# Two of the seven down products made jointly for two column sets, with x of the second half parked in DRAM and Exp and Silu run in order

## The chip, the cores and the metric

The kernel runs on one core of one Trainium2 chip. The time of a run is the device time of one execution in microseconds. I quote medians of the fast runs. PE is TensorE, DVE is VectorE, ACT is ScalarE, POOL is GpSimd and SP is SyncE, whose queue issues the DMAs here. A profiled execution has a "span", from the first to the last instruction that the profile counts. It is about 1.7 us shorter than the time of the same execution (727.4 against 729.12 for the kernel before). The core alone is used, so there is no second die to compare with.

## The reference, cut to what matters

```python
x = A_x                                   # 2048 x 1024, bf16
xn = _layernorm(x)
# A: linear attention, 32 heads of 32
qkv = xn @ wqkv
pq, pk = phi(q), phi(k)                   # phi(t) = where(t > 0, t + 1, exp(t)) + 1e-6
o = (pq @ (pk^T v)) / (pq . sum(pk) + 1e-6)
s = o @ wo
# B: gated feed-forward, F = 3584
h = silu(xn @ w_gate) * (xn @ w_up)
g = silu(h @ w_down)                      # the "down" product: 2048 x 3584 by 3584 x 1024
return x + s * g
```

There are two activation functions with a lookup table, Exp (in phi, for q and k) and Silu (for gate and for the final g).

## The kernel before: the parts that the change touches

The kernel works in two halves of 1024 rows. In each half it makes q, gate and up products, then the down product in four column sets of 256 columns. Every product is a Strassen-type scheme: a 2 x 2 block product is made with seven block products instead of eight, from sums of the weights and sums of the activations. In a column set of the down stage each of the seven is a chain of 14 matmuls of 512 columns into a PSUM bank (PSUM, `ps` in the traces, is the memory that the matmuls write; the kernel uses eight banks of 128 x 512 values).

```python
class Set:                                 # one column set: seven products (cut)
    def step(self, m):
        if m == 1:
            a = balloc(True); self.grp(1, a, True); self.put1(a)
        elif m == 5:
            e = balloc(True); self.grp(5, e, True); self.put5(e)
        elif m == 6:
            self.grp(6, self.b, False)
            self.c = balloc()
            tt([bank_r[self.b], self.s5.r], [bank_r[self.c]], ps[self.c][:, :],      # the DVE add that
               self.s5.ap(F32), ALU.add)                                             # product 3 waits for
        elif m == 3:
            self.grp(3, self.c, False); self.out(0, 1, self.c)
        ...                                # [cut: 2, 7, 4]
```

(The code here is condensed, and comments are mine.) In q, gate and up, products 1 and 5 of two neighbouring sets were already made jointly, as one product of twice the width that is itself split into seven "inner" products (class `Joint`, steps a to d). The down stage made all seven products of each set by itself:

```python
            dset = Set(dops, keep(gv, ACT.Silu), dd_ring)
            seq = "1 5 6 2 7 3 4"
            if link:                       # last set of the first half: woven into the turn to the second half
                seq = "1 5 X 6 nj1a 2 nj1b 7 nj1c 3 nj1d nj5a 4 nj5b n2_0 nj5c n6_0 n2_1 nj5d n6_1"
```

The kernel plans itself at build time. Each operation is recorded with an estimated duration, and a list scheduler fixes the order of every engine's queue. `LEAD=12.0` says how many microseconds ahead of its deadline a load may be issued. `WINDOW=6` says from how many matmul groups, counted from the first one not yet placed, the planner may choose TensorE's next. Once built, every queue runs strictly in order.

```python
def build_kernel(nc, A_x, ..., out, WINDOW=6, NWARM=14, NPE=4, LEAD=12.0):
```

## Time and profile before

| | before |
|---|---|
| time, median of 3 runs | 729.06 us (728.75 to 730.27) |
| PE busy | 712.1 of 727.4 us |
| DVE, ACT busy | 612.7, 400.2 us |
| loads of an activation table | 10, of 1283 ns each |
| DMA | 94.02 MB |

These are lines from the first and fourth part of the page of the kernel before: the busy time of each engine with its instruction count, and the shares of the chain of work that ended last.

```profile
span 727.4 us, 10731 instructions
...
PE 712.1 (98%) x3928; PEld 372.0 (51%) x3942; DVE 612.7 (84%) x1443; ACT 400.2 (55%) x759; POOL 14.4 (2%) x35
...
PE 92%; DVE 4%; ACT 1%; DMA 1%; issue 0%; SPq 0%; DVEq 0%
```

TensorE is busy for 98% of the span, and the chain runs through it for 92%. Where the small remainder sits is seen by stretches. Each row below gives a window in us, its length, then the busy time (and the count) of PE, PE weight load, DVE, ACT and POOL, the granted clock, the DMA share and GB/s.

```profile
337.00:420.00 83.00, 83.00 (x393) 38.22 (x391) 59.22 (x118) 14.67 (x26) 0.00 (x0) 1.00 0.66 166
420.00:445.00 25.00, 24.59 (x142) 13.50 (x141) 22.95 (x60) 19.20 (x34) 0.00 (x0) 1.00 0.51 150
520.00:540.00 20.00, 18.83 (x103) 9.60 (x102) 19.98 (x49) 15.48 (x32) 0.00 (x0) 1.00 0.34 107
636.00:721.00 85.00, 84.84 (x394) 38.28 (x391) 49.35 (x95) 14.53 (x26) 0.00 (x0) 1.00 0.55 132
```

337 to 420 is the down stage of the first half, 420 to 445 the turn, 636 to 721 the down stage of the second half. In the two down stages PE is idle for 0.00 and 0.16 us. In 420 to 445 the gap is 0.41 us. The waits of PE after 200 us, from the view of waits (engine, what it made, what it waited for, total us, how often, the longest):

```profile
PE ps L226 <- DVE TM L360: 1.1, 1, 1.1
PE ps L219 <- DVE ps L360: 0.9, 2, 0.5
PE ps L219 <- ACT ps L350: 0.9, 1, 0.9
PE ps L219 <- ACT TM L350: 0.8, 2, 0.6
PE ps L219 <- DVE W L360: 0.2, 1, 0.2
```

Together 3.9 us, of which the 1.1 us in the first line is the tail of the program. So the kernel is bound by the columns that TensorE streams, and only fewer columns can gain much.

The timeline of PE (start us, length us, engine, line, what, form, count) gives what a 512-column product costs:

```profile
636.07 18.29 PE L219 MATMUL ps<-H,W 128*128 128x512 f16 x84
654.20 3.18 PE L219 MATMUL ps<-P,W 128*128 128x512 f16 x14
657.22 1.03 PE L219 MATMUL ps<-H,W 128*128 128x512 f16 x4
```

From 636.07 to 657.22 there are 98 matmuls: 21.15 / 98 = 0.216 us each. (The length of a row includes the modelled end of its last matmul, so the distance from start to start is what counts. Some records can be missing, which is why I count over whole products.)

### The profile page before, as it was taken

The numbers are of one execution on the slowest core, as the hardware profiler recorded it, in microseconds if no ns is written. First come the engines' busy times: TensorE is split into PE (matmuls) and PEld (weight loads), VectorE is DVE, ScalarE is ACT, GpSimd is POOL, SyncE is SP. The second block draws the span as 40 slices with busy tenths as digits, with TensorE's granted clock in tenths as the row PEclk, the third lists the DMA queues.
The fourth block names the chain that finished last, engine by engine and source line by source line (L and its number), as shares of the span: only waits on it lengthen the run. The fifth ranks groups of instructions, "written<-read, shape, count | busy, mean of one in ns | idle before, by whom it ended". The sixth has DMA issues, their size and how long they took to land.

```text
span 727.4 us, 10731 instructions
## 1 busy us (share of the span) xinstructions
PE 712.1 (98%) x3928; PEld 372.0 (51%) x3942; DVE 612.7 (84%) x1443; ACT 400.2 (55%) x759; POOL 14.4 (2%) x35
## 2 busy tenths in 40 slices
PE   7999999999999999999999999999999999999996
PEld 3544445555555555554444455555555555544442
DVE  5999968989989998888656989999999888875662
ACT  3777654887659666663111267666966756511111
POOL 3111000000000000000000000000000000000000
PEclk9999999999999999999999999999999999999999
DMA  9444235144255343325179655234615344448732
GB/s 295 110 87 102 45 115 174 59 127 149 81 164 156 112 148 114 108 59 151 54 180 253 159 152 160 60 115 119 176 59 187 104 129 131 131 123 188 183 99 51
DMA packets 135668, 94.02 MB, mean 129 GB/s; under 512 B 32960, under 2 KB 131520, under 8 KB 135616
## 3 DMA queue, kind: packets, MB, share of 16 engines
q1 hardware_dynamic: 135616, 93.34, 45.8%
q8 instruction: 31, 0.51, 0.3%
q14 instruction: 21, 0.17, 0.1%
HBM read 75.50 MB, written 10.62 MB: 118 GB/s over the span
## 4 chain that ended last, share of the span: by engine, by line
PE 92%; DVE 4%; ACT 1%; DMA 1%; issue 0%; SPq 0%; DVEq 0%
PE ps L219 92%; DVE H L360 2%; DMA H<-in_A_wqkv_dram 1%; DVE W L360 1%; DVE ps L360 1%; ACT TM L350 1%; ACT L350 0%; SPq L363 0%; DVE TM L360 0%; PE ps L226 0%; ACT ps L350 0%; ACT X L350 0%; DVE H L737 0%; ACT H L350 0%; DVEq L243 0%
## 5 line engine op out<-in xcount | busy, mean ns | idle before, releaser
L219 PE MATMUL ps<-X,W 128*128 128x512 f16 (+1 forms) x1232 | 267.6, 358 | 1.9 <-DVE ps L360 0.9
L350 ACT ACTIVATE TM<-ps 128x512 f16<-128x512 f32 (+2 forms) x345 | 183.6, 553 | 128.5 <-PE ps L219 126.2
L219 PE MATMUL ps<-H,W 128*128 128x512 f16 (+2 forms) x1162 | 250.4, 369 | 0.3
L360 DVE TENSOR_TENSOR W<-W 128x256 f16<-128x256 f16 (+5 forms) x440 | 176.8, 439 | 8.8 <-DMA W<-in_B_w_down_dram 5.8
L219 PEld LDWEIGHTS ps<-H,W 128*128 128x128 f16 (+1 forms) x1168 | 113.9, 98 | 123.4 <-DVE W L360 0.3
L219 PEld LDWEIGHTS ps<-X,W 128*128 128x128 f16 (+1 forms) x1232 | 119.7, 98 | 100.5 <-ACT ps L350 2.1
L360 DVE TENSOR_TENSOR ps<-ps,TM 128x256 f32<-128x256 f32 (+1 forms) x234 | 124.2, 533 | 25.7 <-PE ps L219 23.9
L350 ACT ACTIVATE ps<-ps 128x512 f32<-128x512 f32 (+1 forms) x164 | 81.7, 499 | 108.2 <-PE ps L219 103.6
L219 PE MATMUL ps<-P,W 128*128 128x512 f16 (+1 forms) x496 | 100.1, 329 | 0.6 <-ACT TM L350 0.6
L350 ACT ACTIVATE H<-ps 128x512 f16<-128x512 f32 (+1 forms) x126 | 75.0, 604 | 42.7 <-PE ps L219 42.6
L360 DVE TENSOR_TENSOR H<-H 128x1024 f16<-128x1024 f16 (+4 forms) x106 | 66.5, 642 | 2.2 <-DMA H<-in_A_wqkv_dram 1.9
L219 PEld LDWEIGHTS ps<-P,W 128*128 128x128 f16 (+1 forms) x496 | 48.4, 98 | 31.7 <-ACT TM L350 0.9
L360 DVE TENSOR_TENSOR H<-H,TM 128x512 f16<-128x512 f16 x112 | 44.7, 418 | 15.1 <-ACT H L350 14.9
L219 PE MATMUL ps<-W 128*128 128x256 f16 (+1 forms) x278 | 56.5, 289 | 0.4 <-ACT TM L350 0.2
L350 ACT ACTIVATE TM<-TM 128x512 f16<-128x512 f32 (+1 forms) x61 | 38.0, 627 | 33.9 <-DVE TM L360 33.8
L360 DVE TENSOR_TENSOR TM<-ps,TM 128x512 f32<-128x512 f32 (+1 forms) x60 | 40.8, 680 | 16.2 <-PE ps L219 15.4
L219 PEld LDWEIGHTS ps<-W 128*128 128x128 f16 (+1 forms) x278 | 26.2, 98 | 26.9 <-ACT TM L350 1.5
L219 PE MATMUL ps<-H,X 128*128 128x512 bf16 (+1 forms) x133 | 32.2, 379 | 2.8 <-ACT X L350 1.6
L219 PE MATMUL ps<-TM,W 128*128 128x256 f16 (+1 forms) x138 | 27.8, 283 | 0.1
L360 DVE TENSOR_TENSOR H<-ps,TM 128x512 f16<-128x512 f32 (+1 forms) x35 | 23.9, 683 | 2.3 <-PE ps L219 1.8
L219 PE MATMUL ps<-H,P 128*128 128x512 bf16 (+1 forms) x94 | 23.1, 379 | 0.1
L219 PEld LDWEIGHTS ps<-H,X 128*128 128x128 f16 x136 | 12.7, 98 | 18.3 <-ACT X L350 2.0
(81 smaller groups left out, 392.8 us busy)
## 6 DMA issues: line engine op xcount, KB each, us to landing
W<-in_B_w_down_dram SPq DMA_DIRECT2D x16, 896.0 KB, 6.1
W<-in_B_w_gate_dram SPq DMA_DIRECT2D x12, 1024.0 KB, 5.4
W<-in_B_w_up_dram SPq DMA_DIRECT2D x12, 1024.0 KB, 5.4
W<-in_A_x_dram SPq DMA_DIRECT2D x16, 256.0 KB, 3.0
H<-in_A_wqkv_dram SPq DMA_DIRECT2D x8, 512.0 KB, 8.1
H<-r_scratch SPq DMA_DIRECT2D x32, 128.0 KB, 3.3
W<-m_scratch SPq DMA_DIRECT2D x4, 1024.0 KB, 5.5
s_scratch<-TM SPq DMA_DIRECT2D x32, 128.0 KB, 2.7
```

What stands on the lines that cost most here:

```text
L219: last = h.matmul(o, l, r, start=st, stop=sp, skip_group_check=True)
L350: q = PL.op("act", reads, writes, lambda h: h.activation(o, i, func, **kw), nel(o) / (1000.0 if "bias" in kw or not isinstance(kw.get("sca ...
L360: return dve(reads, writes, lambda h: h.tensor_tensor(o, a, b, op), nel(o), 1.92 if fast else 0.96)
```

## The change

The intent is to save columns. In the down stage, products 1 and 5 of two column sets become one joint product each, made in seven inner products of 7 matmuls of 256 columns. For a pair of sets that is 98 matmuls of 256 columns in place of 56 of 512. It needs inner sums of the weights, inner sums of the activations (`tj_first`, `tj_second`, `tj_last`), and room for both. The room comes from the place `P` that held x of the second half: that is written to DRAM early and loaded back at the turn. A term of product 4 is now made once for two sets. And since Exp and Silu alternate at the turn, `PL.table` forces the runs of the two functions to stay in program order. Some further edits are not shown. Among them, several small tiles moved, and the planner gives vector and scalar work recorded from `END_D` on a deadline 4 us behind its place in TensorE's work instead of 30.

The diff below is cut to its core; comments are mine.

```diff
+    def table(self, o, tab):
+
+        o.tab = tab
+        if self.run and self.run[0].tab != tab:
+            self.past, self.run = self.run, []
+        o.after = [p for p in ([self.run[0]] if self.run else self.past) if p not in o.preds]
+        for p in o.after:
+            p.succs.append(o)
+        self.run.append(o)
 ... [cut]
+        def tj_first(p, u0, u1):                    # sums of the activations for joint product 1
+            B = {(k, j): hq("R00", k, j, u0, u1) for k in range(2) for j in range(2)}
+            t = {m: tq(at, u0, u1) for m, at in TJ1[p].items()}
+            sub(t[7], B[1, 1], B[0, 1])
+            sub(t[5], B[0, 1], B[0, 0])
+            sub(t[6], B[1, 1], t[5])
+            sub(t[4], B[1, 0], t[6])
 ... [cut: tj_second, tj_last, the places of all these]
+        class Down:                                 # two column sets at once
+            def __init__(self, p, h):
+                self.sets = [Set(partial(self.ops, w), self.keep(w), dd_ring) for w in range(2)]
+                self.joint = {"1": Joint(partial(self.jops, 1), lambda w, b: self.sets[w].put1(b)),
+                              "5": Joint(partial(self.jops, 5), lambda w, b: self.sets[w].put5(b))}
+            def jops(self, m, k):
+                ...
+                return [(wa[:, u, :], xa[:, u, :]) for u in range(NU)], [wr, xr]      # 7 of 256 columns
 ... [cut]
-            seq = "1 5 6 2 7 3 4"
-            if link:
-                seq = "1 5 X 6 nj1a 2 nj1b 7 nj1c 3 nj1d nj5a 4 nj5b n2_0 nj5c n6_0 n2_1 nj5d n6_1"
+        IN_D = "7_0 3_0 7_1 3_1 H nj1a 4_0 nj1b 4_1 nj1c n2_0p nj1d n2_0q nj5a n2_1p nj5b n2_1q nj5c n6_0 nj5d"
+        ON_D = "L 7_0 K0 6_1 7_1 K1 nj1a 3_0 nj1b 3_1 S nj1c 4a nj5a nj1d 4b nj5b n2_0 nj5c n2_1 nj5d n6_0"
+        OUT_D = "7_0 3_0 X 6_1 7_1 nj1a 3_1 nj1b nj1c 4a nj5a nj1d 4b nj5b n2_0 nj5c n6_0 n2_1 nj5d n6_1"
+        END_D = "7_0 6_1 7_1 3_0 3_1 4_0 4_1"
 ... [cut]
         def turn_pass():
 
+            for q in range(4):
+                dma([named("xscr", q)], [P.reg(q * 4 * KB, 4 * KB)], P.at(q * 4 * KB, 4 * KB, FP16), x_scr[q],
+                    dsem("xl%d" % q), 512 * KB)
             combos(XV[1])
             x_inner(XV[1])
 ... [cut]
+                if (p, k, n) == (0, "g", 1):
+                    for q in range(4):
+                        dma([P.reg(q * 4 * KB, 4 * KB)], [named("xscr", q)], x_scr[q], P.at(q * 4 * KB, 4 * KB, FP16),
+                            dsem("xp%d" % q), 512 * KB, after=PL.lastpe)
```

## The prediction

> **What bounds the kernel now.** TensorE. The page has PE busy 712.1 of 727.4 us (98%) at clock 0.999, and the chain of waits puts 92% on matmuls. By 20-us windows, PE idles about 4.5 us at the start, 6.2 us at the end (the last product ends about 720.8), and only some 4.5 us between: about 1.3 near 230–238, 1.2 near 525–529, 0.4 at the turn between the halves (420–426). In the down stage (337–420 and 636–721) PE never idles and DVE is busy only 35–75%. So only fewer matmul columns, or those small idles, can save time.
>
> **What a matmul costs here.** In the timeline the down stage issues one 512-column product every 0.216 us (98 from 636.07 to 657.22); 256-column products come every 0.109 us (six from 517.13 to 517.79). This is N/2.4 GHz plus 2.5 ns as in the Trainium skill, "TensorE: Matmul & The Clock Gate", section "Wait — 56ns, not 53.3ns?", and the trace agrees. The weight load (98 ns) still hides under 109 ns, so narrow products lose nothing.
>
> **Removed.** Before, products 1 and 5 of two column sets are 4 x 14 = 56 matmuls of 512: 12.08 us. After, each of the two is 7 inner products of 7 matmuls of 256: 98 x 0.109 = 10.66 us. Saved: 1.42 us per pair of sets, four pairs: 5.7 us, all on the critical path because PE is gapless there. The other five products are unchanged. T4 is made once for two sets: 28 DVE subtractions of 1024 fewer (28 x 0.68 = 19 us of DVE).
>
> **Added, off the path if it fits.** DVE: 32 weight sums of 896 (0.62 each, 20 us), sums of the activations (estimate 15–20 us in all), 16 joint evictions of 256 (0.42, 7 us); net +20 to +30 us: 613 to 635–645. ACT: 16 more narrow copies (0.38, 6 us), minus some of the ten table loads (1.28 us each). Three of the ten sit at 421–428, where Silu and Exp alternate; ordering them should leave one, for at most a few tenths of PE idle. DMA: 4 MB for x, out and back, against 94 MB.
>
> **Moved, and the risks.** Weights of the next two sets go into places just freed; S5, the inner sums and joint 5 follow each other closely, as does x reloaded, summed and used at the turn. DVE in the gate/up stage is already 85–100% busy and gets the first activation sums. A late load or sum costs PE some tenths to 1 us at each of five seams. The tail (Silu, multiply, transposition, add, output) is the same, near 6.5 us.
>
> **Predicted.** 729.1 − 5.7 (columns) − 0.3 (turn) + 0.6 (seams) = 723.7 us; range 721.0 to 727.0. Chances: faster by over 2% 0.01, within 2% 0.97, slower by over 2% 0.02.
>
> **What would show it.** PE busy near 706–707; each down stage about 2.8 us shorter; 224 fewer matmuls of 512 columns and 392 more of 256; spacing still 0.216 and 0.109; six to eight table loads; the start to about 225 us unchanged; the tail within 0.5 us. Wrong if: new PE waits for DVE W or DMA W in the down stage of over 1 us each; a wait for P (x from DRAM) at the turn; 256-column spacing above 0.115; or larger idles near 230 and 525 because the activation sums joined the busy DVE.

## More of the kernel before

At the end, the SyncE queue waits once on every DMA semaphore the program used:

```python
        for s in semn.values():
            if id(s) in PL.count:
                prog["sp"].append(("w", s, PL.count[id(s)]))
```

## The result, and the profile after

The changed kernel takes 726.97 us (median of 4 runs, 726.47 to 727.45), against 728.90 us (728.33 to 730.27, 4 runs) for the kernel before. The ratio is 0.9971, with a 95% interval of 0.9953 to 0.9988. (A ratio is the mean time of one kernel's fast runs over that of the other's of the same rounds, so it is not quite the ratio of the medians I quote.) The gain is about 2 us. I had forecast 5.4.

The same parts of the page and the same windows, after the change:

```profile
span 725.4 us, 11190 instructions
...
PE 707.0 (97%) x4096; PEld 387.4 (53%) x4110; DVE 633.8 (87%) x1501; ACT 402.7 (56%) x773; POOL 14.2 (2%) x35
...
PE 87%; DVE 8%; DMA 2%; ACT 1%; issue 1%; SPq 0%; DVEq 0%
```

```profile
337.00:420.00 83.00, 82.01 (x478) 46.29 (x477) 67.89 (x141) 18.27 (x37) 0.00 (x0) 1.00 0.70 178
420.00:445.00 25.00, 23.54 (x133) 12.31 (x131) 24.60 (x66) 16.98 (x31) 0.00 (x0) 1.00 0.53 147
520.00:540.00 20.00, 18.54 (x103) 9.49 (x101) 19.93 (x46) 19.04 (x38) 0.00 (x0) 1.00 0.45 128
636.00:719.00 83.00, 81.89 (x468) 45.31 (x466) 58.44 (x118) 17.69 (x33) 0.00 (x0) 1.00 0.56 136
```

PE work fell by 5.1 us (712.1 to 707.0), but the time in which PE is idle rose from 15.3 to 18.4 us. PE idle in the windows, which is the length less the first busy figure, went from 0.00 to 0.99 in the first down stage, from 0.41 to 1.46 at the turn, from 1.17 to 1.46 at 520 to 540, and from 0.16 to 1.11 in the second down stage. The matmul count rose by 168 (3928 to 4096), which is exactly 392 narrow ones more and 224 wide ones fewer. The chain's share on PE fell from 92% to 87%, and DVE's rose from 4% to 8%.

The waits of PE after 200 us:

```profile
PE ps L233 <- DVE ps L376: 3.6, 6, 1.0
PE ps L233 <- ACT ps L365: 1.8, 2, 0.9
PE ps L240 <- DVE TM L376: 1.2, 1, 1.2
PE ps L233 <- DVE W L376: 0.3, 1, 0.3
```

The sum is now 6.9 us, 3.0 more than before. The line that grew most is the wait for `ps` written by DVE: from 2 waits and 0.9 us to 6 waits and 3.6 us. The spacing of the narrow products, from the timeline of PE in the second down stage:

```profile
639.55 0.93 PE L233 MATMUL ps<-H,W 128*128 128x256 f16 x7
640.31 0.93 PE L233 MATMUL ps<-X,W 128*128 128x256 f16 x7
641.08 4.71 PE L233 MATMUL ps<-H,W 128*128 128x256 f16 x28
...
656.03 4.28 PE L233 MATMUL ps<-H,W 128*128 128x512 f16 x19 [0.37 <-DVE ps L376]
```

Seven products of 256 columns take 0.76 to 0.77 us from start to start (639.55 to 640.31, 640.31 to 641.08), so 0.109 each, as predicted. The last row shows one of the new waits: PE stood 0.37 us by the profile, waiting for DVE. Counted from start to start it lost 0.54.

To see where the time went without being misled by modelled ends, I use three landmarks that both programs pass: the first matmul of the attention denominators in the first half (landmark 1), the last of those in the second half (landmark 2), and the end of the last product before the closing transpositions. The tail is what is left from there to the end of the span. All later tables have these columns, in us, computed from the start times in the trace.

| profiled run | landmark 1 | 1 to 2 | 2 to the last product | tail | span |
|---|---|---|---|---|---|
| before | 187.83 | 299.87 | 232.98 | 6.73 | 727.4 |
| after | 187.01 | 299.96 | 231.14 | 7.28 | 725.4 |
| after, profiled again (a2_again) | 187.52 | 298.74 | 231.15 | 7.27 | 724.7 |

The first down stage and the turn lie in "1 to 2", the second down stage in "2 to the last product". Each should have shrunk by half of 5.7 us, that is by 2.85. They shrank by 1.13 and 1.83 in the second profile. (In the first, "1 to 2" even grew by 0.09.) The tail grew by 0.54. So 1.7 us were given back between landmarks 1 and 2 (2.9 in the first profile), most of it at the turn, 1.0 in the second half, and 0.54 at the end. The start before landmark 1 scatters by about 0.8 us whatever the kernel, with the landing of the first loads, so its small gain is luck.

The difference between the two profiles of the same kernel is one wait of 1.1 us at 415.94. Here is the chain of waits of the first profile, in order of time, around it:

```profile
390.64 8.01 DMA P<-x_scratch
...
415.55 0.35 DVE ps L376
...
415.94 4.07 PE ps L233 x23
```

A load of x from DRAM took 8.01 us to land, and from there to 415.94 the chain is vector work, mostly the sums of that x (the rows left out). This is the queue of SyncE at that time, and then the row of DVE with the last output additions before it:

```profile
390.10 0.98 SPq L379 DMA_DIRECT2D P<-x_scratch  x2
...
391.59 7.28 SPq L379 DMA_DIRECT2D out_dram<-TM  x3
398.92 1.51 SPq L379 DMA_DIRECT2D P<-x_scratch  x1
```

```profile
390.41 0.75 DVE L376 TENSOR_TENSOR TM<-TM 128x512 bf16<-128x512 f16 x2
```

The chain goes through the second of the four x loads, issued at 390.64. It and the first one landed after 8.0 and 7.3 us; in a2_again, issued at the same place in the queue, after 6.3 and 3.9. So in the first profile x came late because these two loads were slow to land. The DMA engines were about fully busy in both (a share of 0.95 from 393 to 399, and of 1.01 from 392 to 398 in a2_again). Why the loads were slower in one execution stays open.

The three output stores behind them took 7.28 us to issue, and the third x load, which needed nothing, was issued only at 398.92. The stores did not wait for their data: the plan, rebuilt from kernel.py, has them wait for the additions in the DVE row, which ended by 391.17. But they do not make the wait at 415.94 either. In a2_again they took 5.58 us, the third load was issued at 397.76, and PE did not wait.

The second feature is there in every execution, at 438 to 443. These are PE and DVE rows of the timeline of the first profile:

```profile
437.28 1.28 ACT L365 ACT_TABLE_LOAD   x1
437.28 1.03 PE L233 MATMUL ps<-X,W 128*128 128x512 f16 x4
...
438.35 0.70 DVE L376 TENSOR_TENSOR ps<-ps,TM 128x512 f32<-128x512 f32 x1
438.57 1.09 ACT L365 ACTIVATE TM<-ps 128x512 f16<-128x512 f32 x2
438.96 0.68 DVE L755 SCALAR_TENSOR_TENSOR H<-ps,TM 128x512 bf16<-128x512 f32 x1
...
439.11 1.04 PE L233 MATMUL ps<-X,W 128*128 128x512 f16 x4 [0.80 <-DVE ps L376]
...
439.55 0.28 DVE L376 TENSOR_TENSOR W<-W 128x256 f16<-128x256 f16 x1
439.75 0.69 DVE L376 TENSOR_TENSOR ps<-ps,TM 128x512 f32<-128x512 f32 x1
...
440.50 1.04 PE L233 MATMUL ps<-X,W 128*128 128x512 f16 x4 [0.36 <-DVE ps L376]
```

PE makes product 6 (437.28), DVE adds it to a kept partial sum (438.35, 0.70 us), and only then does PE make the next product (439.11), with nothing else to do in between. The second wait, at 440.50, is of another kind: its add began only at 439.75, when DVE had done an operation of phi that reads a PSUM bank (438.96) and a sum of weights (439.55). A third wait of 0.47 us, at 442.93, is for an inner sum of weights.

### The profile page after: what moved, and what is told of

Its sections match the earlier page's. It is cut to its first block, busy times and chain, and to the rows that moved or that the text cites. A ratio compares the mean times of both kernels' runs of the same rounds, so it can differ in the third digit from the quotient of the medians.

```text
span 725.4 us, 11190 instructions
## 1 busy us (share of the span) xinstructions
PE 707.0 (97%) x4096; PEld 387.4 (53%) x4110; DVE 633.8 (87%) x1501; ACT 402.7 (56%) x773; POOL 14.2 (2%) x35
## 2 busy tenths in 40 slices
DMA packets 139127, 98.25 MB, mean 135 GB/s; under 512 B 33344, under 2 KB 136000, under 8 KB 139072
## 4 chain that ended last, share of the span: by engine, by line
PE 87%; DVE 8%; DMA 2%; ACT 1%; issue 1%; SPq 0%; DVEq 0%
PE ps L233 87%; DVE W L376 2%; DVE H L376 2%; DVE X L376 1%; DMA P<-x_scratch 1%; DMA H<-in_A_wqkv_dram 1%; DVE ps L376 1%; DVE TM L376 1%; SPq L379 0%; DVE P L376 0%; ACT TM L365 0%; ACT H L365 0%; PE ps L240 0%; ACT L365 0%; ACT ps L365 0%
## 5 line engine op out<-in xcount | busy, mean ns | idle before, releaser
L233 PE MATMUL ps<-X,W 128*128 128x512 f16 (+1 forms) x1344 | 289.9, 354 | 3.2 <-DVE ps L376 2.3
L233 PE MATMUL ps<-H,W 128*128 128x512 f16 (+2 forms) x1090 | 218.4, 351 | 0.7 <-DVE ps L376 0.4
L376 DVE TENSOR_TENSOR W<-W 128x1024 f16<-128x1024 bf16 (+5 forms) x416 | 184.9, 479 | 5.5 <-PE ps L233 4.9
L233 PEld LDWEIGHTS ps<-X,W 128*128 128x128 f16 (+1 forms) x1344 | 130.4, 98 | 108.6 <-DVE ps L376 4.6
L233 PEld LDWEIGHTS ps<-H,W 128*128 128x128 f16 (+1 forms) x1096 | 106.6, 98 | 95.6 <-DVE ps L376 1.4
L376 DVE TENSOR_TENSOR ps<-ps,TM 128x256 f32<-128x256 f32 (+1 forms) x250 | 130.7, 525 | 13.8 <-PE ps L233 12.5
L233 PE MATMUL ps<-P,W 128*128 128x256 f16 (+1 forms) x516 | 99.8, 319 | 1.2 <-ACT ps L365 0.9
L376 DVE TENSOR_TENSOR H<-H 128x1024 f16<-128x1024 f16 (+6 forms) x110 | 68.9, 640 | 1.1 <-DMA H<-in_A_wqkv_dram 1.0
L233 PEld LDWEIGHTS ps<-H,X 128*128 128x128 f16 (+1 forms) x150 | 14.2, 98 | 18.5 <-ACT X L365 2.0
L376 DVE TENSOR_TENSOR TM<-TM,W 128x512 f16<-128x512 f16 (+1 forms) x39 | 14.1, 362 | 11.5 <-ACT TM L365 11.4
```

The source lines that it names most:

```text
L233: last = h.matmul(o, l, r, start=st, stop=sp, skip_group_check=True)
L376: return dve(reads, writes, lambda h: h.tensor_tensor(o, a, b, op), nel(o), 1.92 if fast else 0.96)
```

## The experiments

My theories for the lost 3.3 us (4.5 in the first profile) were these. Theory A: x comes back late from DRAM. Theory B: the forced order of Exp and Silu holds PSUM banks too long. Theory C: the added vector work fills DVE, so its adds come late. After these fell or shrank, a fourth remained. Theory D: around the seams TensorE's fixed queue has no independent matmul group within its reach of six, so the bare latency from product to add to product is exposed. (In the expectations of e6 to e8 and of e11, "theory D" is an earlier idea: that queues in fixed order pass on a wait at a shared output place.)

All 18 runs follow. In every group the kernel before ran beside the experiments, on their chip. Its medians were 729.11 (chip 6), 729.01 and 728.68 (chip 2), 728.78 (chip 4) and 728.81 us (chip 11).

### Group 1: four single causes

**e1_x_early.** The x loads get a deadline 30 us earlier, which lets them pass the stores.

```diff
                 dma([named("xscr", q)], [P.reg(q * 4 * KB, 4 * KB)], ..., x_scr[q],
-                    dsem("xl%d" % q), 512 * KB)
+                    dsem("xl%d" % q), 512 * KB).urgent = 30.0
```

> The changed kernel with one edit: the four loads that bring x of the second half back from DRAM get a deadline 30 us earlier, so that they stand earlier in the DMA queue. Measured as the time from the first reciprocal product (ps<-H,Zh) of the first half to the last of the second: 299.9 us before, 300.0 after, and 2.85 less than before if the joint products were pure gain. Theory A (x comes back late, all its sums then crowd the vector engine at the turn): this interval falls by 1.5 to 2.5 us, to about 298, and the matmul waits at 416 and 439-443 (2.4 us together) shrink to under 1 us; time near 725. Theory B (Exp in order after Silu frees PSUM late): interval within 0.5 us of 300.0. Theory C (too much vector work at the turn, whenever x comes): within 0.7 us of 300.0.

Measured: 730.59 us, ratio 1.0017 [0.9993, 1.0042] to the kernel before, so the whole gain was gone. "1 to 2" grew to 302.14. DVE's timeline shows what happened:

```profile
403.98 0.43 DVE L376 TENSOR_TENSOR TM<-TM 128x512 bf16<-128x512 f16 x1 [0.96 <-DMA TM<-TM]
...
405.92 0.42 DVE L376 TENSOR_TENSOR TM<-TM 128x512 bf16<-128x512 f16 x1 [0.51 <-DMA TM<-in_A_x_dram]
...
409.68 0.70 DVE L376 TENSOR_TENSOR ps<-ps,TM 128x512 f32<-128x512 f32 x1
```

Now that the sums of x come early in DVE's fixed order, the output additions of the first half stand among them, and DVE stops for a transposition by DMA (0.96 us) and for a load of x into a shared place (0.51 us). The add that PE needs begins only at 409.68. The row of PE, and the windows around it:

```profile
410.43 5.75 PE L233 MATMUL ps<-H,W 128*128 128x512 f16 x18 [2.45 <-DVE ps L376]
```

```profile
408.00:410.50 2.50, 0.07 (x1) 0.07 (x2) 2.50 (x6) 0.66 (x2) 0.00 (x0) 1.00 0.49 112
410.50:414.00 3.50, 3.50 (x9) 1.22 (x10) 2.74 (x5) 0.00 (x0) 0.00 (x0) 0.51 0.16 32
```

PE stood for 2.45 us, and then ran at half clock (0.51) for 3.5 us. Eight wide matmuls there came about 0.43 us apart instead of 0.216, which cost another 1.7 us. The Trainium skill, "TensorE: Matmul & The Clock Gate", section "Wait — 56ns, not 53.3ns?", gives 426.7 ns for a cold 512-column matmul, and the trace agrees. Theory A in its simple form, "earlier x is better", falls.

**e2_x_fill.** The x loads are replaced by a fill with a constant by POOL. The result is wrong. (A first form without any writer was not run: it would have read values that nobody had written.)

```diff
-                dma([named("xscr", q)], [P.reg(...)], P.at(...), x_scr[q], dsem("xl%d" % q), 512 * KB)
+                pool([], [P.reg(...)], lambda h, q=q: h.memset(P.at(...), 0.5), 2.2)
```

> The changed kernel without the load of x from DRAM: the idle GpSimd writes the constant 0.5 into its four places as soon as they are free. The result of the second half is wrong on purpose; all its sums and products remain. Theory A: interval between the reciprocal products falls from 300.0 to 297.3-298.2, matmul waits between 405 and 446 below 0.8 us, time 724.5 to 725.3. Theory B: interval 299.5 to 300.3. Theory C: 299.3 to 300.3.

Measured: 729.70 us, ratio 1.0011, "1 to 2" 301.07, with one wait of 3.2 us at 410.7. Even with no DRAM load at all the turn is slower. The first sum of x now stands at 387.90 in DVE's queue (390.29 in e1, 398.68 in the changed kernel), so the planner had again moved the sums forward, among the output chain. Removing the wait for x is not enough. None of the three theories had forecast this.

**e3_free_tables.** The order of Exp and Silu is set free again.

```diff
         o.tab = tab
+        return
         if self.run and self.run[0].tab != tab:
```

> The changed kernel with the rule that Exp and Silu run in order taken out (the scheduler may mix them as before). Theory B: the matmul waits at 439-443 (1.5 us) go, interval 298.0 to 298.8, time near 725.5. Theories A and C: waits at the turn are as large or larger, 10 to 12 table loads in place of 8, interval 300 to 301.5, time 727 to 728.5.

Measured: 733.46 us, ratio 1.0064 [1.0052, 1.0076]. There are 12 table loads instead of 8. "1 to 2" grew from 299.96 to 304.58, with waits of 3.2, 0.9 and 2.05 us at 442 to 446. PE also ran at a granted clock of 0.52 from 446.3 to 449.5. Theory B is refuted in the form that I tested: setting the order free does not take the waits away. In the changed kernel the order is worth more than 4 us, in a plan made anew. My prediction had given it "a few tenths".

**e4_joint_second.** Joint products only in the second half, with no dump and no reload of x. The program has an error: in the first half the place of x also serves as room for weight sums in this version, so its result is wrong. The amounts of work and the order are as meant, so I use its time with that reserve.

```diff
+        JOINT = (False, True)
...
-                    self.joint[t[1]].step("abcd".index(t[2]))
+                    if JOINT[self.p]:
+                        self.joint[t[1]].step("abcd".index(t[2]))
+                    elif t[2] in "ab":
+                        self.sets["ab".index(t[2])].step(int(t[1]))
```

> The changed kernel with joint products in the second half only: in the first half products 1 and 5 are made as before (56 matmuls of 512 each pair of sets), and x of the second half stays in SBUF; the new places, the shared T4, the order of Exp and Silu remain. Theory A and C: the first half's joint products gained nothing net, so the interval is 299.5 to 300.5 and the time that of the changed kernel within 0.7 us (726.3 to 727.6). Theory B: the waits at 439-443 remain without the gain: interval 301.5 to 302.5, time near 729.

Measured: 728.71 us, ratio 0.9996. "2 to the last product" is 231.15, the same as in the changed kernel, so the second half took the same time however the first half made its products. "1 to 2" is 300.66, so 0.8 above the kernel before, with waits of 0.52 at 410 and 1.01 at 444. No x comes from DRAM here. So part of the turn's loss belongs to the new order of products and not to x. The interval lies between my two forecasts and the time near that of theory B, so e4 decides for neither.

### Group 2: the order alone, a place of its own, and thinner vector work

**b1_order_only.** The kernel before, with only the ordering of Exp and Silu added (the `table` method of the diff above).

> The kernel before with one part of the change alone: Exp and Silu run in order. The kernel before mixes them at the turn (10 table loads, matmul waits of 0.73 us there). If the order is worth what it looked like in the run without it (6 us), it is because of the fuller vector engine of the changed kernel; here I expect 8 table loads, interval between the reciprocal products 299.0 to 300.2 (299.9 before), time 728.0 to 729.3. If the order as such is worth much: interval under 298.5.

Measured: 728.84 us, ratio 0.9997. There are 8 table loads instead of 10, and every landmark distance is the same as before (299.87, 232.98, 6.73). The two spare loads had cost PE nothing. So the ordering gives nothing alone, and several us in company with the joint products (e3).

**e6_own_place** and **e7_own_place_early.** e1 failed at a place that two transfers share. e6 gives the last x tile of the output its own place, in rows of `H` that are free then. e7 adds the earlier x of e1.

```diff
-                    q = xo_rings[self.link].take()
+                    q = Spread() if self.link and (w, j) == (1, 1) else xo_rings[self.link].take()
...  (e7 only)
-                    dsem("xl%d" % q), 512 * KB)
+                    dsem("xl%d" % q), 512 * KB).urgent = 30.0
```

> The changed kernel, but the fourth output tile of the last column sets of the first half gets a place of its own (in dead columns of h) in place of sharing one with the third, so that its load of x does not wait for the third's store. Theory D (the in-order queues pass that wait on: store, load, add, and the next eviction behind the add): alone it does little, as x from DRAM comes late all the same: interval 299.0 to 300.5, time 726.3 to 727.6. Theory A alone: 300.0 within 0.5.

> The same with x of the second half loaded early (the earlier run x early lost 2.6 us in one wait at 410 and a slower clock after it). Theory D: the wait at 410 falls below 1 us, no slow clock, interval 297.8 to 299.0, time 724.7 to 726.3: faster than both kernels. Theory C (volume of vector work): interval stays 300 to 302.

Measured: e6 727.46 us (ratio 0.9980, "1 to 2" 299.87), e7 726.70 us (0.9971, 298.37). Compared with the second profile of the changed kernel (298.74), e7 gains 0.4 us in the profile and nothing in the time. It still waits 0.70 us at 407.7 and 1.01 at 441. Against e1, though, the wait near 410 fell from 2.61 us to 0.70 and no slow clock followed, so the shared place was most of what e1 lost. So theory A accounts for about 1.1 us in those executions where x lands late, and for no more.

**e8_thin_out.** About 5 us of vector work of the output chain at the turn is made almost free by working on a few columns only. The result is wrong.

```diff
-                tt([g.r, sf.r], [g.r], g.ap(FP16), g.ap(FP16), sf.ap(FP16), ALU.mult, True)
+                if self.link:
+                    dve([g.r, sf.r], [g.r], lambda h: h.tensor_tensor(
+                        g.ap(FP16)[:, 0:4], g.ap(FP16)[:, 0:4], sf.ap(FP16)[:, 0:4], ALU.mult), 512, 1.92)
...  (the same for the addition)
```

> The changed kernel with every instruction in the same order, but the output multiply and add of the last column sets of the first half work on 4 and 8 columns in place of 512 (result wrong on purpose): about 5 us less vector work between 375 and 430, nothing else. Theory C (the vector engine is full from 398 to 446 and its volume is what the matmuls wait for): the waits at 416 and 439-443 (3.1 us) fall to under 1.2 us, interval 297.5 to 298.7, time 724.8 to 725.9. Theories A and D (late arrivals): waits fall by less than 1 us, interval 299.2 to 300.2.

Measured: 726.69 us, ratio 0.9968. "1 to 2" is 298.73. The waits after 438 did not move:

```profile
438.45 1.04 PE L233 MATMUL ps<-X,W 128*128 128x512 f16 x4 [0.80 <-DVE ps L376]
439.85 1.04 PE L233 MATMUL ps<-X,W 128*128 128x512 f16 x4 [0.36 <-DVE ps L376]
```

They read 0.80 and 0.36, exactly the 0.80 and 0.36 of the same rows in the changed kernel (439.11 and 440.50). My first reading was that thinning had removed the wait at 415.9. The repeat of the unchanged kernel (a2_again below) has no such wait either, so that reading was wrong. Theory C is refuted for the vector work of the output chain. The other vector work at the turn (phi, the sums of x and of weights) was not thinned in any run, and the add at 439.75 did stand behind some of it.

### Group 3: the end, the second seam, and the lead

**e9_place_early_end.** e7, and the last two sets finish one after the other instead of interleaved, to look at the tail.

```diff
-        END_D = "7_0 6_1 7_1 3_0 3_1 4_0 4_1"
+        END_D = "7_0 3_0 4_0 6_1 7_1 3_1 4_1"
```

> The version with x loaded early and a place of its own for the fourth output tile, and with the last eight products of the program ordered so that one column set is finished before the other (7 3 4 6 of set 0 first, then 7 3 4 of set 1) in place of alternating. The changed kernel's tail after the last product is 7.3 us, the kernel before has 6.7, with three stores in a row in the DMA queue in place of two. If that is why: tail 6.5 to 6.9, interval between the reciprocal products 298.4 as in the run without this edit, time 726.0 to 726.6 (0.5 under that run). If the tail has another cause: 7.2 to 7.5.

Measured: 728.39 us, ratio 0.9994. Two new waits of 0.96 us came in, at 697.1 and 710.2. ("2 to the last product" grew to 232.88.) The tail stayed long, 7.47. So the order of the end is not what makes the tail long, and the interleaving of the change hides 1.9 us of product, add, product.

**e10_thin_second_seam.** The sums of the activations for joint product 5 of the second half are thinned. The result is wrong.

```diff
+            if thin:
+                dve([a[1], b[1]], [o[1]], lambda h: h.tensor_tensor(
+                    o[0][:, :, 0:4], a[0][:, :, 0:4], b[0][:, :, 0:4], ALU.subtract), nel(o[0]), 1.92)
+                return
```

> The changed kernel, every instruction in the same order, but in the second half the column sums for joint product 5 (seven vector instructions, about 5.8 us) work on a few columns only (result wrong on purpose). If the vector engine's volume makes the matmul waits at the start of the second down stage (0.68 us at 636-656): they fall below 0.2 us, time from the last reciprocal product to the last product falls from 231.1 to 230.4-230.7. If a latency of the chain makes them: unchanged.

Measured: 726.48 us, ratio 0.9972. The wait at 656 fell from 0.54 to 0.28 us. Theory C is right there, for a quarter of a microsecond.

**e11_lead.** Loads may be issued 18 us ahead instead of 12. Nothing else is edited, but the planner makes a new plan.

```diff
-def build_kernel(..., WINDOW=6, NWARM=14, NPE=4, LEAD=12.0):
+def build_kernel(..., WINDOW=6, NWARM=14, NPE=4, LEAD=18.0):
```

> Control: the changed kernel with the scheduler told to issue loads 18 us ahead in place of 12, which re-plans all orders. It shows how far the waits at the turn move by a new order alone. Theory A and D (late arrivals): x loads stand earlier in the queue, interval 298.3 to 299.8, time 725.5 to 727. If new orders scatter by over 1 us with no relation to when x comes, the interval may be anything from 299 to 302.

Measured: 724.73 us, ratio 0.9953 [0.9937, 0.9968]. "1 to 2" is 297.64, "2 to the last product" 229.42. The waits near 236 and 535, 1.9 us each, shrank to 0.3 each. This is the first edit that gained, and it gained in stages whose products the change had left as they were.

### Group 4: does a wider view give the gain back, and is it the change's own?

**a2_again** is the changed kernel once more. **b2_ahead** is the kernel before and **a3_ahead** the changed kernel, both with a longer lead and a wider reach. **e12_all** is a3_ahead with e7's edits.

```diff
-def build_kernel(..., WINDOW=6, NWARM=14, NPE=4, LEAD=12.0):
+def build_kernel(..., WINDOW=14, NWARM=14, NPE=4, LEAD=22.0):
```

> The changed kernel once more, unedited. If the wait of 1.1 us at 416 belongs to every execution: interval between the reciprocal products 300.0. If it depends on when x lands in that execution: 298.7, as in the two runs with the same first half, with the waits at 429-443 (2.1 us) and 656 (0.54) as before. Time 726.3 to 727.3.

> The kernel before, with loads issued up to 22 us ahead in place of 12 and matmul groups reordered within 14 in place of 6. The waits at 236-238 (1.7 us) go; those at the turn (0.7) and at 526-528 (1.7) shrink. Time 725 to 727, so 2 to 4 us of the run with loads 18 us ahead were not the change's.

> The changed kernel with the same two settings. If its lost gain went into waits for late loads and for short independent work, they shrink more here than in the kernel before: time 720.5 to 722.5, difference to b2_ahead 4 to 5 us, most of the 5.7 us that the columns are worth. If the change costs as much under any settings: difference 2 us.

> The same with x early and the fourth output place: interval between reciprocal products near 296.5, time 720 to 722; equal to a3_ahead within 1 us, as loads 22 us ahead already bring x early.

| run | time, median | ratio to before [95%] | 1 to 2 | 2 to the last product | tail |
|---|---|---|---|---|---|
| a2_again | 726.62 | 0.9969 [0.9957, 0.9982] | 298.74 | 231.15 | 7.27 |
| b2_ahead | 726.34 | 0.9966 [0.9953, 0.9978] | 299.10 | 232.12 | 6.89 |
| a3_ahead | 720.91 | 0.9892 [0.9878, 0.9905] | 296.31 | 228.68 | 7.27 |
| e12_all | 721.15 | 0.9897 [0.9882, 0.9912] | 295.29 | 228.69 | 7.74 |

With the wider view the change is worth 726.34 − 720.91 = 5.4 us, close to the 5.7 us of its columns. With the narrow view it is worth 2.2 (728.78 − 726.62). The waits of PE in a3_ahead:

```profile
PE ps L240 <- DVE TM L376: 1.1, 1, 1.1
PE ps L233 <- DVE ps L376: 0.7, 1, 0.7
PE ps L233 <- DMA X<-in_B_w_up_dram: 0.3, 1, 0.3
PE ps L233 <- DVE X L376: 0.2, 1, 0.2
```

The matmuls and the vector work are nearly those of the changed kernel (PE 706.7, DVE 632.7 us busy). The wait for `ps` from DVE fell from 6 waits and 3.6 us (5 and 2.6 in a2_again) to 1 wait and 0.7 us. That fits theory D: the same work, in an order that has something else for PE to do in between. (The orders of DVE and ACT are new as well.)

But most of the gain of the wide view lies elsewhere. Counted from start to start, PE waited as follows, in us, in these profiles:

| waits of PE | before | a2_again | b2_ahead | a3_ahead | e15_ahead_stores_last (plan of a3_ahead) |
|---|---|---|---|---|---|
| near 220 to 240 and 525 to 540, stages whose products the change left as they were | 3.4 | 3.7 | 2.1 | 0.0 | 0.1 |
| starts of the two down stages, and the turn (400 to 447) | 0.7 | 3.0 | 0.2 | 1.9 | 1.0 |

In the first row the wide view took 3.7 us from the changed kernel but only 1.3 from the kernel before. So about 2.4 of the 3.2 us by which it raised the worth of the change (from 2.2 to 5.4) come from there, and I put them down to the luck of two plans. In the second row, the change's own seams, the wide view raised that worth by about 0.5 us (1.4 by the profile of e15, which lacks 0.9 us of waits for a weight load and a sum near 440 that a3_ahead's profile has). So e12's 295.29 for "1 to 2" in the table above shows no gain of its edits: e15, with the plan of a3_ahead, has 295.38. That 5.4 is close to 5.7 does not show that the seams gave their loss back. And the lead and the reach were changed together here. e11 shows that the lead alone gives about 2 us, but no run widened the reach alone.

### Group 5: the tail

What was left open was the tail, longer by 0.54 us although the operations in it are the same. The view of waits of SyncE's queue, kernel before and then kernel after, shows the wait for the last store:

```profile
...
SPq L211 <- DMA out_dram<-TM: 1.1, 1, 1.1
...
```

```profile
...
SPq L225 <- DMA out_dram<-TM: 0.5, 1, 0.5
...
```

That wait got shorter by 0.6 us, while the tail grew. The other thing in the tail is the list of final waits on DMA semaphores, 70 before and 94 after. Three kernels move only the order of this list.

```diff
-        for s in semn.values():
+        for n in sorted(semn, key=lambda n: n.startswith("oo")):      # stores last; "not ..." for stores first
+            s = semn[n]
             if id(s) in PL.count:
                 prog["sp"].append(("w", s, PL.count[id(s)]))
```

**e14_stores_last** is the changed kernel, **e15_ahead_stores_last** is a3_ahead, both with the stores' waits last. **b3_stores_first** is the kernel before, with them first.

> The changed kernel; the final waits on the DMA semaphores are the same 94, only those of the output stores are waited on last, so that the others pass while the last store is in flight. If the passed waits cost time behind the last store (about 20 of them, estimated at 25 ns from the 0.55 us by which the tail grew), the time from the end of the last product to the end falls from 7.28 to 6.3 to 6.8 us, the end to 726.3 us or so. If the tail grew for another reason (a slower store), it stays at 7.2 to 7.4.

> The changed kernel with the longer lead and reach, and the waits on the stores last. Theory of the passed waits: about 0.5 us below the 720.9 us of the same kernel without it, 720.4, tail 6.3 to 6.8. Rival: 720.9, tail 7.2 to 7.4.

> The kernel before, with the final waits on the output stores first, so that 65 passed waits follow the landing of the last store, instead of at most 14. Theory of the passed waits: the tail grows from 6.73 us by 65 times about 22 to 25 ns, to 8.0 to 8.4 us, and the time by about 1.4 us to 730.3. Rival: nothing changes, 6.7 and 728.9.

| run | time, median | ratio to before [95%] | tail | wait instructions after the last store | their spacing | gaps over 0.1 us |
|---|---|---|---|---|---|---|
| before (first profile) | 729.06 | | 6.73 | 35 | 0.061 | one of 1.10 |
| after (first profile) | 726.97 | 0.9971 | 7.28 | 47 | 0.061 | 0.38 and 0.55 |
| e14_stores_last | 725.99 | 0.9963 [0.9948, 0.9977] | 6.79 | 47 | 0.061 | 0.38 |
| e15_ahead_stores_last | 720.36 | 0.9886 [0.9871, 0.9900] | 6.81 | 47 | 0.061 | 0.38 |
| b3_stores_first | 728.15 | 0.9994 [0.9977, 1.0010] | 5.82 | 35 | 0.061 | none |

The right columns come from the records of semaphore instructions in the trace. Each instruction holds two waits, and one passes every 0.061 us, so 94 waits take 47 × 0.061 = 2.9 us even when all are long satisfied. e14 and e15 came out as expected: the tail fell by 0.5 us.

b3 came out against its expectation. The tail did not grow by 1.4 us but shrank by 0.9. The records say why. The semaphore numbers run in pairs from the middle of my list outwards (140 with 138, 141 with 137, and so on, in the kernel before), so the two ends of the list are waited on last, whichever end the stores are at. Putting them first therefore also put them last in the program that runs, and the whole landing of the store was covered by other waits. What I had argued about the cost of a passed wait was right (about 30 ns, two to an instruction). What I had assumed about the order of the list was wrong. One thing stays open: a gap of 0.38 us at the 21st or 22nd wait instruction of every profile of the changed kernel that I counted, and in none of the kernel before.

e15_ahead_stores_last at 720.36 us is the fastest correct kernel, 1.1% below the kernel before.

## Why the prediction was right and where it was wrong

1. **Columns: right.** I had forecast 5.7 us saved on PE, at 0.216 and 0.109 us per matmul. Both spacings were measured again in the changed kernel, and the count changed by exactly +392 and −224. PE busy fell to 707.0, as forecast ("near 706–707"). The difference of busy time is only 5.1 us because every new wait adds a modelled matmul end.

2. **Seams: this is the step that failed.** (A seam is a place where one pair of column sets, or one half, passes over into the next.) The prediction put it as "a late load or sum costs PE some tenths to 1 us at each of five seams" and then entered "+ 0.6 (seams)" in the sum. It measured 2.7 us in the second profile: 1.7 between landmarks 1 and 2, and 1.0 in the second half. (In the first profile it was 3.9, because x landed late.) By the waits counted from start to start, the turn holds 0.96 + 0.52 + 0.47 us of new waits at 439 to 443 and 0.1 at 430, against 0.73 before. Between 337 and 357 there are 0.34 us more, and the second half has 0.68 at 636 to 656. Another 0.2 of the second half is a longer wait near 530, in a stage whose products the change left as they were. The kind of loss was named rightly, but the sum took less than the lower end of the range it had just stated. Five times "some tenths to 1 us" is 1.5 to 5 us, not 0.6.

3. **Why the seams lose: in part open.** I had expected a wait for x from DRAM at the turn. It is real but occurs only in some executions, at 1.1 us. Bringing x earlier alone made the kernel slower (e1, e2). The vector work of the output chain is not it at the turn (e8), and the sums of the activations are it only for 0.26 us at 656 (e10). What the trace shows at 439 is a chain of product, add of 0.70 us, product, with no other matmul in between; at 440.5 and 442.9 it shows an add and a sum of weights that come late in DVE's queue. Whether their amount or their order counts there is not shown. Wider planning leaves one wait of 0.85 us of these 1.95, and none at 656 (a3_ahead; e15, with the same plan). That this is due to the reach of the plan is not isolated, since the lead changed too.

4. **Tail: a wrong step of 0.54 us.** The prediction said "the tail ... is the same, near 6.5 us". The operations are the same. But I had not counted the final waits: 24 more semaphores are 12 more wait instructions, and e14 gets 0.5 us back by reordering them.

5. **Order of Exp and Silu: mis-sized.** I had entered "− 0.3 (turn)". Alone it is worth nothing (b1). In the changed kernel its absence costs more than 4 us (e3), a slow clock included. It is not a gain beside the others but a condition for them.

6. **DVE, ACT, DMA and table loads: right or nearly.** DVE 633.8 us (forecast 635 to 645), table loads 8 (six to eight), DMA 98.25 MB (4 MB more).

With the measured sizes the sum closes. For the second profile: −5.7 + 2.7 (seams and turn) + 0.54 (tail) − 0.3 (start, luck) = −2.7 us, and the spans are 727.4 and 724.7. The forecast range of 721 to 727 held the result at its upper edge, but the middle of it was too low.

## What to carry to other kernels

When work is taken out of a pipeline whose queues are fixed at build time, the gain shows only as far as the plan has independent work to put where the new dependencies wait. So plan the kernel anew with a wider reach before judging such a change, do the same to the kernel before, and look at which waits moved. The comparison is always between two plans: 2.2 us against 5.4 us here, and most of the difference came from stages whose products were the same in both kernels. When a prediction lists several risks of "some tenths to 1 us", add them up at their middle. And look at the last microseconds by instruction: 94 waits, nearly all long satisfied, took 2.9 us, and sorting them gained half a microsecond for one line of code.

## What the Trainium skill lacked or had wrong

- "TensorE: Matmul & The Clock Gate", section "What's actually happening", says the clock falls to half after at least one idle window of about 3.4 us. In e1_x_early PE stood for only 2.45 us and then ran at a granted clock of 0.51 for 3.5 us. An idle time shorter than a window was enough here. But in e2_x_fill PE stood for 3.05 us at the same place, and the clock of the 3.4 us after it was 1.00. In e3_free_tables it stood for 3.00 us, then for 0.56 and 1.73, and the clock was 0.57 from 442.0 to 446.3 and 0.52 from there to 449.5. So the length of the idle time alone does not decide. The page's free-running window may be the reason, but no run here shows where the window lay.
- "ScalarE: Activation LUTs", section "What ACT_TABLE_LOAD costs", gives 1283 ns for the load plus about 1380 ns of drain. The 1283 ns agree (10 loads before, 8 after). The drain does not show as lost time: in the timeline above a load begins at 437.28, and the next activation begins at 438.57, 1.29 us later. And b1 shows that two loads fewer, off the critical path, change nothing.
- No page that I read tells how long the issue of one DMA can hold SyncE's queue when its data is ready. Three stores took 0.87, 1.73 and 4.59 us to issue at 391.59 to 398.88 of the changed kernel, while the DMA engines were about fully busy; the next one, at 402.42, took 0.43. No run here shows the cause.
- No page that I read gives the cost of a wait that is already satisfied. On SyncE two such waits share an instruction and pass in 0.061 us, and the program that runs had them in pairs from the middle of the source's list outwards.
